# A linear-attention and gated-convolution kernel: negated filter spectrum read from PSUM, sign flips moved to VectorE, zero matmuls in pauses, and a new written-out order

## The chip, the cores and the metric

The kernel runs on one core of one Trainium2 chip. The metric is the device time of one execution in microseconds (us); the median of three executions is compared. TensorE (PE) does the matmuls, VectorE (DVE), ScalarE (ACT) and GpSimd (POOL) the elementwise work, and SyncE (SP) issues nearly all transfers.

## What is computed

The reference runs two blocks one after the other. Sizes are 4 batches, 8 heads, 768 time steps and head width 48, so a row of all heads is 384 wide.

```
for t in range(S):                                   # linear attention with decay
    cur = einsum('bhd,bhe->bhde', u * k_t, v_t)
    y[t] = einsum('bhd,bhde->bhe', r_t, state + cur)
    state = w_t[..., None] * state + einsum('bhd,bhe->bhde', k_t, v_t)
proj = y @ w_proj                                    # 384 -> 3 * 384: x1, x2, x3
x2_conv = irfft(rfft(x2, axis=time) * rfft(filter_fft, axis=time), n=S)
out = (x1 * x2_conv * x3) @ w_out
```

## The kernel before

The time axis is cut into chunks of 128 steps, six per batch, 24 in all (chunk 0 to 23). Loads and a part of the elementwise work go by group: chunks 0 and 1 alone, then pairs. For each chunk the names below are one operation each; a number behind the name is the chunk or the group.

- `lw`, `lk`, `lr`, `lv` (line 1244) are SyncE's loads of w, k, r and v, 192 KB each in runs of 192 bytes. `ln` (line 1250) is the logarithm of w on ScalarE. `vb` casts v to bf16.
- `rk`, `ru`, `rh`, `cc`, `vc` (lines 1158, 1260, 1263) make the bonus term: r times k, times u, a halving sum, a sum over the head, and that sum times v. They are spread over GpSimd and VectorE.
- `cs` (lines 1278 to 1281) sums the logarithms on TensorE, `ex` (1284) is the exponential on ScalarE in place in PSUM, `kq` (1287) multiplies with k and r on VectorE, `ph` (1291) is the decay of the whole chunk. `tr` (1299) transposes, `qk` copies the result out of PSUM (ScalarE or VectorE), `sc` (1311) are the scores, `mt` (1327, or a plain copy by line 1162) takes them out of PSUM with or without the causal mask, and `mc` (1332) cuts the triangle on GpSimd where `mt` was a plain copy.
- `ki`, `kv`, `su` (1358, 1352, 1362) carry the state to the next chunk: `su` on VectorE writes the state that `ys` (1381) of the next chunk reads. `yi`, `ys`, `y` add bonus, state part and scores part in PSUM; `xn` takes the sum out of PSUM (where `yi` is left out, `xn` on VectorE adds the bonus, line 1401); `yt` transposes and `xT` copies out.

For each batch the second block follows as soon as its rows are there: `xw` (1573) is the middle projection in natural layout and `cxw` its copy, `sd` (1584) folds the two halves of time, `f` (1438) is the forward transform with the sine table `F`, `cf` its copy to `X`. `p` and `q` (1536) are the other two projections: `cp` copies the first, `cq` (1561) makes their product, the gate `g`. `u` and `p` with two numbers (1158, 1610) multiply with the filter's spectrum `hh`. `E` (1628) is the inverse transform with the table `mi` and its sign-flipped copy `mx`, `cE`, `aE`, `dE`, `yE` put the halves together and multiply with the gate, `o` (1692) is the last projection, `co` its copy, `so` (1708) the store.

Three pieces are made once, in the first half of the run. The tables come from sines (`ang`, `ia`, `sin`, `is`). `if` (`flips`, lines 1481 to 1486) makes four sign-flipped copies of `mi` on GpSimd. The filter is loaded by `filt` (1495), folded by `fsd0` and `fsd1` (1498, VectorE, tile `P`), transformed by `h1`, `h2`, `h0` (1438), copied out of PSUM with its scale by `hc` on ScalarE (1504, tile `hh`), and `hg` (`gcopy`, lines 1508 to 1516) on VectorE makes the second copy and the negated one from the bf16 tile `hh`.

The order of all work is written out by hand in the table `ORDER`: one line per operation with its engine's letter (P TensorE, A, N ScalarE, D, V, M VectorE, G, C GpSimd, S SyncE, - for left out) and its PSUM bank. Each engine runs its own operations strictly in this order and waits at each for its inputs and its bank. A third word ties a GpSimd operation behind a VectorE one, if that one's function returns its instruction. `warm n` are n matmuls of a zero tile (line 1193).

Of the kernel before, what the change touches and what calls it, by code (L numbers as in the profile page):

```python
# [21 lines left out]
L = 128  # L22
NCH = S // L
C = H * D
# [13 lines left out]
ADD, DVE2, ACT2, POOL2, FOLD = "V", "M", "N", "C", "Q"  # L38
# [6 lines left out]
wz D  # L45
maps G
lw0 S
lr0 S
lk0 S
warm 30 7  # L50
lk1 S
lw1 S
smalls D
pads D
imaps G
ia0 G
kz3 D
kz1 D
ang2 D
u S  # L60
ang1 D
lw2 S
lw3 S
ang0 D
lr1 S
lr2 S
ia2 D
ia1 D
# [3 lines left out]
trig A  # L72
sin2 A
sin1 A
sin0 A
is A
table A
ln1 A
masks G ang0
ln0 A  # L80
rk0 G
ur D
um P 0
kz0 D
ub D
lv0 S
kz2 G ia2
cs1 P 4
rk1 G ia2
cs0 P 2  # L90
ln2 A
ex1 A
ru0 D
rh0 D
cc0 D
ex0 A
kq1 D
cs3 P 6
ex3 A
ph1 A  # L100
kq0 D
cs2 P 0
ex2 A
tr1 P 5
ph0 A
tr0 P 4
qk1 A
# [108 lines left out]
xn2 A
yt2 P 3
xT2 D
vb3 G su3
kv4 P  # L220
sc5 P 5
mt4.0 A
cc3 D
xT3 A
mt4.1 A
xw0.2 P 3
mt5.0 D
mt5.1 D
su4 D
mc4.1 G  # L230
cxw0.2 A
xw0.0 P 0
filt S
vc3 G xT2
yi5 P 5
mc5.1 -
ln4 A
cxw0.0 D
lv7 S
mc4.0 G mt5.0  # L240
yi4 P 3
ys5 P
ys4 P
y4 P
mc5.0 -
xn4 A
y5 P
xn5 D
cs6 P 0
lv6 S  # L250
lw9 S
yt4 P 2
xT4 D
yt5 P 5
xT5 D
cs7 P 3
ex6 A
lw8 S
ex7 A
kq6 D  # L260
xw0.4 P 6
kq7 D
ph6 A
cxw0.4 A
lk8 S
lr9 S
lv8 S
tr6 P 5
qk6 D
tr7 P 0  # L270
ph7 A
lr8 S
qk7 A
lk9 S
sd0.0.0 D
sc6 P 2
mt6.1 -
f0.0 P 6
lk10 S
wproj0 G  # L280
lv9 S
lw10 S
p0.2.1 P 4
p0.2.0 P 5
cf0.0 A
mt6.0 N
p0.0.1 P 0
rk4 D
sd0.1.0 D
cp0.2.0 D  # L290
f0.2 P 5
p0.0.0 P 2
cf0.2 A
cp0.0.0 A
sc7 P 6
lr10 S
lr11 S
lw11 S
ru4 D
cp0.0.1 D  # L300
fsd0 D
mc6.0 C
ln5 A
lk11 S
fsd1 D
h1 P 0
mt7.0 M
h2 P 2
lv10 S
mc6.1 -  # L310
rh4 D
cc4 D
mt7.1 -
hc1 A
hg1 D
mc7.0 -
h0 P 6
hc2 A
cp0.2.1 A
vb4 G xT4  # L320
vc4 G fsd0
lw13 S
lv13 S
kv6 P 3
hg2 D
su6 D
mc7.1 -
yi6 - 2
hc0 A
hg0 D  # L330
cs8 P 0
yi7 P 4
wproj2 G
y6 P
ys7 P
ex8 A
y7 P
xn6 V
cs9 P 6
xn7 A  # L340
ki7 P 2
kv7 P
kq8 D
yt7 P 3
yt6 P 5
tr8 P 4
su7 D
lr12 S
lv11 S
ex9 A  # L350
lr14 S
xT6 D
kq9 D
lw12 S
# [651 lines left out]
yE3.2.0 G cq3.2.0
o3.0.1 P
# [783 lines left out]
```

## Time and profile before

| what | before |
|---|---|
| time, median of three executions | 167.73 us (166.23 to 168.83) |
| profiled execution, its own time | 167.69 us |
| its span on the core | 165.9 us |
| mean granted TensorE clock | 0.931 |
| PE busy | 144.2 us (87%), 1665 matmuls |
| VectorE busy | 140.3 us (85%), 259 instructions |
| ScalarE busy | 117.7 us (71%), 192 instructions |
| GpSimd busy | 99.3 us (60%), 103 instructions |
| bytes moved | 26.23 MB, 158 GB/s over the span |

The page gives busy time by engine, then the span in 40 slices of 4.15 us. The view by windows gives the busy time of each engine in a stretch, so that an engine's idle time there is the difference. The waits name who ended the idle time. The profiled execution's own time is 1.79 us over its span.

### The profile page before, as it was taken

How to read it: one execution, taken by the hardware profiler on the slowest of the kernel's cores; microseconds unless marked ns; L12 is line 12 of the kernel's file. 1: busy time of each engine (PE TensorE's matmuls, PEld its weight loads, DVE VectorE, ACT ScalarE, POOL GpSimd, SP SyncE). 2: the span in 40 equal slices, each digit the busy share in tenths (PEclk: the TensorE clock that was granted, in tenths of full speed). 3: DMA queues.
4: the chain of work that ended last, by engine and by line, in shares of the span. 5: the costliest groups of instructions: out<-in, count | busy, mean ns of one | idle time of the engine just before them, and what ended most of it. 6: DMA issues, size and time to landing. Idle time of an engine off the chain costs nothing.

```text
span 165.9 us, 4290 instructions
## 1 busy us (share of the span) xinstructions
PE 144.2 (87%) x1665; PEld 94.9 (57%) x1665; DVE 140.3 (85%) x259; ACT 117.7 (71%) x192; POOL 99.3 (60%) x103
## 2 busy tenths in 40 slices
PE   7868877984984999649999999999989999999980
PEld 5538655652543667344666677667567666655530
DVE  6758999892799889375899999999999999999950
ACT  4997956674274686634998988878989866785460
POOL 7967796602227059985695799699269680330320
PEclk9965999998699599965999999999999999999997
DMA  5999999899999989999999999900250000200936
GB/s 107 212 212 215 207 199 203 161 287 194 211 212 175 203 166 205 184 217 214 201 192 217 191 211 184 175 11 0 96 194 0 4 0 4 95 2 19 356 133 254
DMA packets 104118, 26.23 MB, mean 158 GB/s; under 512 B 100129, under 2 KB 102690, under 8 KB 104098
## 3 DMA queue, kind: packets, MB, share of 16 engines
q1 hardware_dynamic: 102498, 24.78, 68.1%
q0 software_dynamic: 1600, 1.18, 5.0%
q8 instruction: 13, 0.21, 0.5%
q14 instruction: 7, 0.06, 0.1%
HBM read 22.41 MB, written 4.72 MB: 164 GB/s over the span
## 4 chain that ended last, share of the span: by engine, by line
PE 29%; DVE 22%; POOL 15%; DMA 12%; issue 11%; ACT 7%; SPq 1%; POOLq 0%; ACTq 0%; DVEq 0%
PE banks L1536 6%; POOL rk L1158 6%; DMA wproj<-in_moe_w_proj_dram 5%; PE banks L1438 5%; PE banks L1299 4%; DMA out_dram<-o 3%; PE banks L1692 3%; PE banks L1573 3%; POOL mt L1332 3%; DVE kq L1287 3%; PE banks L1628 2%; DVE hh L1514 2%; DMA w<-in_w_dram 2%; DMA kr<-in_k_dram 2%; POOL vc L1158 2%
## 5 line engine op out<-in xcount | busy, mean ns | idle before, releaser
L1536 PE MATMUL banks<-xT,wproj 128*128 128x384 bf16 x144 | 29.8, 344 | 2.7 <-DMA wproj<-in_moe_w_proj_dram 2.1
L1332 POOL TENSOR_SCALAR_AFFINE_SELECT mt<-mt 128x512 bf16<-128x512 bf16 (+1 forms) x17 | 15.9, 937 | 16.5 <-ACT mt L1162 11.8
L1158 POOL TENSOR_TENSOR vc<-vb,cc 128x768 bf16<-128x768 bf16 (+1 forms) x13 | 18.3, 1410 | 10.6 <-DVE cc L1263 7.6
L1287 DVE TENSOR_TENSOR kq<-banks,kr 128x768 bf16<-128x768 f32 x24 | 22.7, 950 | 2.2 <-ACT banks L1284 1.9
L1162 ACT ACTIVATE x<-banks 128x768 bf16<-128x768 f32 (+1 forms) x26 | 18.0, 700 | 6.1 <-PE banks L1573 4.0
L1158 POOL TENSOR_TENSOR rk<-kr 128x768 bf16<-128x768 f32 (+1 forms) x12 | 20.1, 1679 | 2.6 <-DMA kr<-in_r_dram 1.3
L1299 PE MATMUL banks<-ident,kq 128*128 128x128 bf16 x192 | 16.8, 243 | 5.1 <-DVE kq L1287 4.5
L1536 PEld LDWEIGHTS <-wproj 128*128 128x128 bf16 x144 | 13.5, 102 | 11.9 <-DMA wproj<-in_moe_w_proj_dram 2.5
L1284 ACT ACTIVATE banks<-banks 128x768 f32<-128x768 f32 x24 | 19.1, 804 | 0.5 <-PE banks L1281 0.2
L1299 PEld LDWEIGHTS <-kq 128*128 128x128 bf16 x192 | 13.6, 110 | 7.3 <-DVE kq L1287 6.7
L1327 DVE TENSOR_TENSOR mt<-banks,mask_excl 128x512 bf16<-128x512 f32 (+1 forms) x17 | 15.6, 934 | 2.4 <-PE banks L1311 2.0
L1162 ACT ACTIVATE qk<-banks 128x1024 bf16<-128x1024 bf16 x14 | 14.1, 1028 | 2.4 <-PE banks L1299 2.3
L1162 ACT ACTIVATE X<-banks 128x768 bf16<-128x768 f32 x12 | 9.7, 811 | 7.8 <-PE banks L1438 7.5
L1162 ACT ACTIVATE mt<-banks 128x512 bf16<-128x512 f32 (+1 forms) x17 | 12.6, 749 | 3.7 <-PE banks L1311 3.1
L1158 POOL TENSOR_TENSOR y<-y,g 128x768 bf16<-128x768 bf16 (+1 forms) x6 | 8.1, 1354 | 11.6 <-PE banks L1628 9.0
L1438 PE MATMUL banks<-sd,F 128*128 128x384 bf16 (+1 forms) x96 | 14.0, 336 | 0.3 <-DVE sd L1584 0.3
L1573 PE MATMUL banks<-wproj,xT 128*128 128x384 bf16 x72 | 14.0, 333 | 0.1
L1692 PE MATMUL banks<-wout,y 128*128 128x384 bf16 x72 | 13.2, 326 | 0.0
L1438 PEld LDWEIGHTS <-F 128*128 128x128 bf16 (+1 forms) x120 | 9.1, 106 | 7.0 <-issue 2.9
L1561 DVE TENSOR_TENSOR g<-banks,x 128x384 bf16<-128x384 f32 (+1 forms) x16 | 11.6, 747 | 0.2 <-PE banks L1536 0.2
L1162 ACT ACTIVATE o<-banks 128x768 f32<-128x768 f32 (+1 forms) x12 | 9.1, 782 | 3.6 <-PE banks L1692 1.9
L1158 DVE TENSOR_TENSOR U<-X,hh 128x2304 bf16<-128x2304 bf16 (+1 forms) x12 | 11.1, 950 | 0.0
(110 smaller groups left out, 331.0 us busy)
## 6 DMA issues: line engine op xcount, KB each, us to landing
w<-in_w_dram SPq DMA_DIRECT2D x24, 192.0 KB, 3.9
kr<-in_r_dram SPq DMA_DIRECT2D x24, 192.0 KB, 3.8
kr<-in_k_dram SPq DMA_DIRECT2D x24, 192.0 KB, 3.8
v<-in_v_dram SPq DMA_DIRECT2D x24, 192.0 KB, 4.2
out_dram<-o SPq DMA_DIRECT2D x11, 384.0 KB, 3.0
U<-in_moe_filter_fft_dram SPq DMA_DIRECT2D x1, 1152.0 KB, 9.3
wproj<-in_moe_w_proj_dram POOLq DMA_DIRECT2D x3, 288.0 KB, 5.8
out_dram<-o SPq DMA_DIRECT2D x2, 192.0 KB, 2.6
```

Of the source, the lines that this page charges most:

```text
L1158: return eng(e).tensor_mul(o, a, b)
L1162: return nc.scalar.activation(out=o, in_=a, func=AF.Copy)
L1284: op(f"ex{i}", [ACT], lambda e, bk: nc.scalar.activation(out=two(bk, f"cs{i}")[:, :, 0:C], in_=two(bk, f"cs{i}")[:, :, 0:C], func=AF.Exp), ...
L1287: op(f"kq{i}", [DVE], lambda e, bk: nc.vector.tensor_mul(kq[f][:, :, :, 0:D], two(bk, f"cs{i}")[:, :, 0:C].rearrange("p a (h d) -> p a h d ...
L1299: nc.tensor.transpose(p[:, HP * m + j, :], kq[f][:, m, 2 * j:2 * j + 2, :], ident)
L1327: return copy(ACT, o, x) if e in (ACT, ACT2) else nc.vector.tensor_mul(o, x, _mid(mask_excl, z - HP * a))
L1332: return nc.gpsimd.affine_select(out=o, in_=o, pattern=[[0, z - HP * a], [1, L]], compare_op=ALU.is_gt, fill=0.0, base=0, channel_multipli ...
L1438: nc.tensor.matmul(p[rows], F[:, ti, c0 + rows.start:c0 + rows.stop], x[q][:, ti, :], start=(ti == 0), stop=(ti == NT - 1),)
L1536: nc.tensor.matmul(p, wproj[:, cb, col0:col0 + L], xT[bx][:, cb, sl], start=(cb == 0), stop=(cb == CB - 1),)
L1561: op("c" + n3, [DVE], lambda e, bk: nc.vector.tensor_mul(g[bx][:, fs, sl], view(bk, n3), x1[:, fs, sl]), r=[f"x1.{fb}.{hf}" for fb in fbs] ...
L1573: nc.tensor.matmul(view(bk)[:, z], xT[bx][:, cb, (c0 + z) * L:(c0 + z + 1) * L], wproj[:, cb, C:2 * C], start=(cb == 0), stop=(cb == CB - 1),)
L1692: nc.tensor.matmul(view(bk)[:, z], yt_[:, z, :], wout[:, cb, :], start=(cb == 0), stop=(cb == CB - 1),)
```

## The change

Four edits are in the code, and the table of the order is new.

1. `hg` makes the negated part of the spectrum from PSUM instead of from the bf16 tile in SBUF, with the scale in the same instruction; for the first block the scale is a column `neg0`. Its other copies still go from `hh` to `hh`.
2. `if` stands in the table with VectorE's letter, and much earlier.
3. `warm` lines stand at many places: 73 zero matmuls where there were 30.
4. A new letter X takes `xn` out of PSUM on ScalarE into an fp32 tile `xf`, and a new GpSimd operation `xa` adds the bonus. Two chunks use it (18 and 20).

```diff
+    neg0 = sb.tile([L, 1], FP32, name="neg0")
+        nc.vector.memset(neg0, -2.0 / S)
+        nc.vector.memset(neg0[0:1, :], 0.0)
...
-            o = xn[:, i % NX].rearrange("p (j a d) -> p a j d", a=2, d=D)
+            o = (xf if e == WIDE else xn)[:, i % NX].rearrange("p (j a d) -> p a j d", a=2, d=D)
...
-            return copy(e, o, yview(bk))
+            return copy(ACT if e == WIDE else e, o, yview(bk))
...
+        op(f"xa{i}", [POOL, NONE], lambda e, bk: nc.gpsimd.tensor_add(
+            xn[:, i % NX], xf[:, i % NX], vcq.rearrange("p h d -> p (h d)")),
+           r=[f"xn.{i % NX}", f"vc.{fg}"], w=[f"xn.{i % NX}"])
...
                 nc.vector.tensor_scalar(
-                    out=hh[:, 1, 0, n, :], in0=hh[:, 0, 1, n, :], scalar1=-1.0, scalar2=None, op0=ALU.mult)
+                    out=hh[:, 1, 0, n, :], in0=two(bk, f"h{n}")[:, 1, 0:C], scalar1=-2.0 / S if n else neg0,
+                    scalar2=None, op0=ALU.mult)
...
-            op(f"hg{n}", [DVE], gcopy(n), r=[f"Hc.{n}"], w=[f"H.{n}"])
+            op(f"hg{n}", [DVE], gcopy(n), r=[f"Hc.{n}"], w=[f"H.{n}"], uses=[f"h{n}"])
```

Counted over the table, these operations change their engine: `qk` from 14 on ScalarE and 10 on VectorE to 16 and 8; `xT` from 11 and 13 to 17 and 7; `vb` from 7 on ScalarE and 6 on GpSimd to 10 and 3; `vc` from 13 on GpSimd to 11 and 2 on VectorE; `ru` and `rh` together from 15 on VectorE and 11 on GpSimd to 11 and 15; `yE` from 9 on VectorE and 6 on GpSimd to 12 and 3; `dE` from 8 and 4 to 11 and 3.

The first place is GpSimd around the loads of the projection's weights, `wproj` (the first of the two is the middle third, the second the first third). `vc2` and `rk0` belong to chunks 2 and 3 and to 4 and 5. Before:

```order
L1227 DMA wproj_137<-in_moe_w_proj_dram 128x3x384
L1158 TENSOR_TENSOR vc2_87<-vb2_83,cc2_80 128x768
L1158 TENSOR_TENSOR rk0_75<-kr3_67 128x768
L1164 CAST vb3_84<-v3_71 128x768
L1332 AFFINE_SELECT mt1_101<-mt1_101 128x512
L1158 TENSOR_TENSOR vc0_85<-vb3_84,cc0_78 128x768
L1332 AFFINE_SELECT mt1_101<-mt1_101 128x512
L1227 DMA wproj_137<-in_moe_w_proj_dram 128x3x384
```

Now:

```order
L1193 TENSOR_TENSOR vc2_87<-vb2_83,cc2_80 128x768
L1264 DMA wproj_138<-in_moe_w_proj_dram 128x3x384 x2
L1193 TENSOR_TENSOR rk0_75<-kr3_67 128x768
L1297 TENSOR_TENSOR rk0_75<-rk0_75 128x16x24
L1193 TENSOR_TENSOR vc0_85<-vb3_84,cc0_78 128x768
```

The first load moved behind `vc2`, and the second moved up behind it, ahead of `rk0`.

The second place is VectorE around the filter's spectrum: `P` is the folded filter, `hh` the spectrum, `S3` the state that `su6` writes. Before:

```order
L1498 TENSOR_TENSOR P_116<-U_117 128x1152 x2
L1327 TENSOR_TENSOR mt1_101<-banks_152,mask_excl_142 128x1024
L1260 TENSOR_TENSOR rk1_76<-rk1_76 128x16x24
L1263 TENSOR_REDUCE cc1_79<-rk1_76 128x16
L1510 COPY hh_136<-hh_136 128x384
L1514 TENSOR_SCALAR hh_136<-hh_136 128x384
L1510 COPY hh_136<-hh_136 128x384
L1514 TENSOR_SCALAR hh_136<-hh_136 128x384
L1362 TENSOR_TENSOR S3_106<-banks_152,phi2_94 128x192
```

Now:

```order
L1539 TENSOR_TENSOR P_117<-U_118 128x1152 x2
L1300 TENSOR_REDUCE cc1_79<-rk1_76 128x16
L1364 TENSOR_TENSOR mt1_101<-banks_154,mask_excl_143 128x1024
L1551 COPY hh_137<-hh_137 128x384
L1555 TENSOR_SCALAR hh_137<-banks_154 128x384
L1551 COPY hh_137<-hh_137 128x384
L1555 TENSOR_SCALAR hh_137<-banks_154 128x384
L1399 TENSOR_TENSOR S3_106<-banks_154,phi2_94 128x192
```

The negating instruction now reads the PSUM banks; the copies and their place stay.

The third place is VectorE some 10 us of work later, at `kq` of chunks 10 and 11 and the bonus of group 6 (`rk0`). Before:

```order
L1287 TENSOR_TENSOR kq3_91<-banks_152,kr2_66 128x16x48
L1158 TENSOR_TENSOR rk0_75<-rk0_75,u_b_151 128x768
L1287 TENSOR_TENSOR kq2_90<-banks_152,kr2_66 128x16x48
L1610 TENSOR_TENSOR P_116<-U_117 128x2304
L1263 TENSOR_REDUCE cc0_78<-rk0_75 128x16
```

Now:

```order
L1324 TENSOR_TENSOR kq3_91<-banks_154,kr2_66 128x16x48
L1324 TENSOR_TENSOR kq2_90<-banks_154,kr2_66 128x16x48
L1297 TENSOR_TENSOR rk0_75<-rk0_75 128x16x24
L1652 TENSOR_TENSOR P_117<-U_118 128x2304
L1300 TENSOR_REDUCE cc0_78<-rk0_75 128x16
```

The product with u (`ru6`) left VectorE for GpSimd and no longer stands between the two `kq`; the halving sum (`rh6`) came in behind them. GpSimd has the flips no more ahead of that group's `rk`: the four instructions of `if` now stand on VectorE right behind the product with u of chunks 4 and 5.

On TensorE the first projection of batch 0 (`p0.0.0`) now stands ahead of the transposes of chunks 4 and 5, of `xw0.4` and of `cs6`. Zero matmuls stand there in groups of two to six ahead of `xw0.0`, `xw0.4`, `sc6`, `sc7` and `h1`: 34 of them behind the 39 at the start.

More of the change, by code (lines that the diff above doesn't have):

```diff
@@ L45 @@
 wz D
[L46 to L53 removed]
+warm 28 5
+lw3 S
+lr0 S
+lw1 S
+lw0 S
+lk1 S
+trig A
+maps G
 pads D
 imaps G
[L56 to L68 removed]
+ia1 G
+u S
+lr1 S
+kz1 D
+smalls D
+ang2 D
+ang1 D
+ang0 D
+sin2 A
+ia0 D
+masks G ang0
+sin1 A
+lw2 S
+rk1 G ia0
+ia2 D
+lk0 S
+ur D
+um P 6
+warm 11 5
+kz2 D
+ub D
+ru1 D
+sin0 A
+is A
+table A
+kz3 D
 lk3 S
@@ L242 @@
[L242 to L256, printed above, removed]
-ex6 A
-lw8 S
+mt5.0 D
+mc5.0 -
+vc3 G
+warm 6 2
+xw0.0 P 2
+xw0.2 P 4
+mc4.0 C xT3
+rk4 G
+yi4 P 0
+yi5 P 6
+ys4 P
+ys5 P
+mc5.1 -
+y5 P
+lr8 S
+lk9 S
+cxw0.2 A
+mc4.1 -
+y4 P
+lr9 S
+lk8 S
+lv8 S
+lv9 S
+lr10 S
+p0.0.0 P 4
+xn4 A
+xa4 -
+yt4 P 1
+cxw0.0 D
+lw10 S
+lk10 S
+lw11 S
+xn5 D
+xa5 -
+yt5 P 3
+xT4 A
+xT5 D
+warm 3 2
+xw0.4 P 2
+cp0.0.0 D
+cxw0.4 D
+ln4 A
+cs6 P 4
+ex6 A
+sd0.0.0 D
@@ L259 @@
+kq6 D
+p0.2.1 P 7
+cs7 P 0
+p0.0.1 P 2
+cp0.2.1 A
 ex7 A
-kq6 D
-xw0.4 P 6
 kq7 D
 ph6 A
[L264 to L267, printed above, removed]
-tr6 P 5
[L269 to L276, printed above, removed]
-mt6.1 -
[L278 to L285, printed above, removed]
-mt6.0 N
[L287 to L309, printed above, removed]
-mc6.1 -
@@ L311 @@
[L311 to L317, printed above, removed]
-hc2 A
[L319 to L324, printed above, removed]
+cp0.0.1 A
+sd0.1.0 D
+ru4 D
+f0.0 P 6
+lr11 S
+lk11 S
+p0.2.0 P 4
+rh4 D
+cf0.0 A
+ph7 A
+tr7 P 3
+qk7 A
+tr6 P 5
+qk6 A
+cp0.2.0 A
+f0.2 P 6
+cf0.2 A
+lw12 S
+fsd0 D
+fsd1 D
+warm 5 2
+sc6 P 0
+ln5 A
+warm 6 2
+sc7 P 5
+cc4 D
+vb4 G fsd0
+mt7.0 M
+mc7.0 -
+mt7.1 -
+mt6.1 -
+lw13 S
+mt6.0 N
+warm 6 2
+h1 P 2
+h2 P 0
+hc1 A
+h0 P 4
+hg1 D
+mc6.1 -
+hc2 A
 hg2 D
+kv6 P 7
 su6 D
-mc7.1 -
@@ new lines @@
+cp2.0.0 A
+tr18 P 3
+vb10 A
+kq19 D
+ph19 A
+qk18 D
+xw2.2 P 6
+p2.2.0 P 1
+cxw2.2 A
+sc17 P 4
+mt17.1 A
+cp2.2.0 A
+ln11 A
+ru10 D
+mt17.0 D
+mc17.0 -
+vc9 G
+kv18 P 3
+q2.0.0 P 6
+su18 D
+cq2.2.0 D
+lr23 S
+lw23 S
+yi16 - 0
+ys16 P
+sc18 P 4
+mt18.1 -
+o0.0 P 2
+mt18.0 N
+rh10 G ru10
+cc10 D
+cq2.0.0 D
+co0.0 A
+mc16.1 G su18
+y16 P
+xn16 V
+xa16 -
+cs20 P 4
+mc17.1 G cq2.2.0
+tr19 P 6
+qk19 D
+yt16 P 3
+ex20 A
+mc18.1 -
+yi17 - 6
+o0.1 P 0
+vc10 G
+vb11 A
+mc18.0 C
+co0.1 A
+ys17 P
+y17 P
+xT16 D
@@ new lines @@
+sc19 P 2
+kq20 D
+mt19.1 -
+mc19.1 -
+ki19 P 1
+kv19 P
+xn17 V
+xa17 -
+ph20 A
+rk11 G
+yt17 P 7
+mt19.0 N
+tr20 P 4
+su19 D
+u01.0 D
+cs21 P 0
+ru11 D
+xT17 A
+qk20 A
+lw22 S
+rh11 G
+p1.0 D
+ex21 A
+xw2.4 P 5
+cxw2.4 A
+o0.2 P 2
+so0.0 S
+co0.2 A
+kq21 D
+p2.2.1 P 7
+ki20 P 6
+kv20 P
+su20 D
+sc20 P 4
+cp2.2.1 A
+p2.0.1 P 2
+q2.2.1 P 7
+mt20.0 D
+ln12 A
+mt20.1 A
+ph21 A
+cp2.0.1 A
+cs22 P 4
+ex22 A
+mc19.0 C
+tr21 P 6
+cc11 D
+yi18 - 2
+sd2.1.0 D
+lk23 S
+lk22 S
+y18 P
+mc20.0 -
+xn18 X
+q2.0.1 P 0
```

1279 lines of the change are left out of this document (592 added, 687 removed).

## The prediction

> **What bounds the kernel now.** I read the slices first, then the busy time by windows, then what VectorE waited for, and last the instructions around the long waits.
>
> ```profile
> PE   7868877984984999649999999999989999999980
> DVE  6758999892799889375899999999999999999950
> PEclk9965999998699599965999999999999999999997
> DMA  5999999899999989999999999900250000200936
> ```
>
> A slice is 4.15 us. Up to slice 25 (108 us) the transfers never pause, yet they are not what ends last: from slice 19 on TensorE and VectorE are both full, and they stay full for 58 us after the last input. Holes stand only before, at slices 8 to 10, 12, 13 and 16 to 18.
>
> ```profile
> core 0: us, PE busy (x) PEld busy (x) DVE busy (x) ACT busy (x) POOL busy (x), PEclk, DMA share, GB/s
> 12.00:33.30 21.30, 17.93 (x300) 13.89 (x299) 18.91 (x35) 15.28 (x29) 16.08 (x18) 0.89 1.04 197
> 33.30:80.25 46.95, 37.40 (x386) 23.27 (x385) 34.89 (x50) 27.34 (x44) 23.49 (x19) 0.85 1.03 206
> 80.25:161.70 81.45, 79.95 (x933) 52.11 (x931) 78.75 (x140) 65.54 (x109) 50.57 (x40) 1.00 0.47 112
> 50.90:54.30 3.40, 1.08 (x26) 0.87 (x26) 3.24 (x7) 0.89 (x2) 1.85 (x2) 1.00 1.10 169
> 54.30:57.70 3.40, 3.05 (x31) 2.24 (x27) 2.96 (x6) 2.13 (x4) 0.00 (x0) 0.50 1.13 215
> 68.00:71.40 3.40, 1.23 (x8) 0.52 (x6) 0.04 (x1) 1.08 (x2) 3.33 (x3) 1.00 1.07 209
> 71.40:78.20 6.80, 5.36 (x47) 3.53 (x47) 4.74 (x7) 3.23 (x5) 4.58 (x4) 0.50 1.10 217
> ```
>
> The run has three stages. In the last, from `kq` of chunk 12 at 80.25 us to the end of VectorE's work, TensorE is busy 79.95 of 81.45 us: nothing is to be had there but by taking work away. The middle one, 33.30 to 80.25, has 12.06 us without VectorE (46.95 less 34.89) and 9.55 without TensorE. So the question is how much earlier chunk 12 starts, and whether the last stage keeps its length. These are VectorE's waits in the middle stage:
>
> ```profile
> DVE x L1164 <- PE banks L1536: 4.0, 2, 3.1
> DVE rk L1158 <- POOL rk L1158: 3.7, 1, 3.7
> DVE mt L1327 <- PE banks L1311: 1.8, 1, 1.8
> DVE qk L1164 <- PE banks L1299: 0.3, 1, 0.3
> ```
>
> **The change part by part.**
>
> *a. The projection's weights.* The 4.0 us are `cp`, waiting for `p0` on TensorE, which waits for a transfer that GpSimd issues; the chain of waits has it as one piece of 8.62 us.
>
> ```profile
> 31.08 8.62 DMA wproj<-in_moe_w_proj_dram
> 24.19 1.82 POOL L1158 TENSOR_TENSOR rk<-kr 128x768 bf16<-128x768 f32 x1
> 30.78 0.88 SPq L1495 DMA_DIRECT2D U<-in_moe_filter_fft_dram  x1
> U<-in_moe_filter_fft_dram SPq DMA_DIRECT2D x1, 1152.0 KB, 9.3
> 43.91 2.62 DVE L1498 TENSOR_TENSOR P<-U 128x1152 bf16<-128x1152 f32 x2
> ```
>
> The changed order issues it ahead of the `rk` that starts at 24.19, so about 25 instead of 31; even at 8.62 us it lands by 34, when `p0.0.0` comes up. What is late next is the filter: issued at 30.78 and 9.3 us under way, it is there at 40.1 (estimate), so the fold `P` can move from 43.91 to 40.1 at best: 3.8 us. The changed order also puts `cp0.0.0`, `cxw0.4` and `sd0.0.0` ahead of `kq6`, some 2.5 us of work that VectorE had done behind it. I take 2.5; ends 0 (the weights are as late as before) and 3.8.
>
> *b. The negated spectrum.* On VectorE and GpSimd:
>
> ```profile
> 48.59 0.26 DVE L1510 COPY hh<-hh 128x384 bf16<-128x384 bf16 x1
> 48.77 1.53 DVE L1514 TENSOR_SCALAR hh<-hh 128x384 bf16<-128x384 bf16 x1
> 50.39 2.51 DVE L1514 TENSOR_SCALAR hh<-hh 128x384 bf16<-128x384 bf16 x1
> 52.82 0.34 DVE L1362 TENSOR_TENSOR S<-banks,phi 128x192 bf16<-128x192 f32 x1
> 53.96 0.26 DVE L1514 TENSOR_SCALAR hh<-hh 128x384 bf16<-128x384 bf16 x1
> 48.66 1.52 POOL L1158 TENSOR_TENSOR vc<-vb,cc 128x768 bf16<-128x768 bf16 x1 [5.91 <-DVE cc L1263]
> 50.96 1.81 POOL L1158 TENSOR_TENSOR rk<-kr 128x768 bf16<-128x768 f32 x1
> L1164 DVE CAST xn<-banks 128x384 bf16<-128x384 f32 x2 | 1.1, 552 | 0.1
> ```
>
> One and the same instruction takes 0.26 us where GpSimd is idle and 1.53 and 2.51 where `vc` and `rk` run: it ends at 50.30 and 52.90, just after they do (50.18 and 52.77). The two engines shut each other out there, for 3.5 us in sum. The state `S` stands behind it, and TensorE's pause from 50.90 to 54.30 follows from that. Read from PSUM, the nearest row of the size is 0.55, so three cost 0.9 more than 0.26 each: the gain is 2.6 if PSUM frees it, and 0 if the copies ahead of it, still from `hh` to `hh`, get shut out in its place. I take 2.4, nearer to the upper end since the one copy quoted took 0.26 with `vc` starting 0.07 later.
>
> The Trainium skill, SBUF — State Buffer, "Who interferes with whom", says the same of the lock, that the loser waits for the whole instruction; but it counts copies from SBUF among the instructions that contend. By that rule the four copies left in `hg` and the moved flips are as exposed as before; that is a rival below.
>
> *c. The flips.* GpSimd's rows:
>
> ```profile
> 64.73 1.25 POOL L1482 TENSOR_SCALAR mi<-mi,sgn 128x384 bf16<-128x384 bf16 x1
> 65.97 2.45 POOL L1484 TENSOR_SCALAR mx<-mi,sgn 128x384 bf16<-128x384 bf16 x2
> 68.40 1.16 POOL L1486 TENSOR_SCALAR mi<-mi 128x384 bf16<-128x384 bf16 x1
> 69.53 1.79 POOL L1158 TENSOR_TENSOR rk<-kr 128x768 bf16<-128x768 f32 x1
> 71.36 0.56 DVE L1158 TENSOR_TENSOR rk<-rk,u_b 128x768 bf16<-128x768 bf16 x1 [3.68 <-POOL rk L1158]
> ```
>
> The flips hold GpSimd for 4.9 us; `rk6` comes behind, VectorE's `ru6` waits 3.7 us for it, and `kq10` stands behind `ru6`. Without the flips `rk6` is done about 5 us sooner, and `ru6` has left that queue. I take the 3.7 whole. On VectorE four flips cost 1.0 at 0.26 each, and at most 8 at the 1.53 to 2.51 beside a busy GpSimd (estimate). They stand before `kq6`, where VectorE would wait for the filter in (a) anyway, so I count nothing; with that cover gone it is 1 to 2.
>
> *d. The clock.* At 54.30 and 71.40 the clock is granted at 0.50, each after a stretch in which TensorE worked 1.08 or 1.23 of 3.40 us. From 71.40 on, VectorE's waits for scores and transposes (1.8 and 0.3) and some small ones are of that half speed. Where b and c take the pauses away, no slow stretch follows: 2.3 us; ends 0 and 2.7, half of TensorE's 5.36 there. The Trainium skill, TensorE: Matmul & The Clock Gate, "What's actually happening", puts the fall after a whole idle window of some 3.4 us. This trace differs: about 1.1 busy of 3.40 was enough. By the rule alone zero matmuls would be needless in pauses as short as these.
>
> *e. Zero matmuls.* At the start 30 of them took 6.1 us:
>
> ```profile
> L1193 PE MATMUL banks<-wt 128*128 128x256 bf16 x30 | 6.1, 394 | 1.1 <-DVE scl L1208 1.1
> L1162 ACT ACTIVATE qk<-banks 128x1024 bf16<-128x1024 bf16 x14 | 14.1, 1028 | 2.4 <-PE banks L1299 2.3
> L1162 ACT ACTIVATE xT<-banks 128x384 bf16<-128x384 bf16 x11 | 5.3, 492 | 1.8 <-PE banks L1409 1.8
> L1162 ACT ACTIVATE vb<-v 128x768 bf16<-128x768 f32 (+1 forms) x7 | 5.6, 802 | 0.0
> ```
>
> That is 0.20 each at the slow start, so the 34 behind the start are at most 6.8 us. Seventeen stand before `sc6`, `sc7` and `h1`, where TensorE waits for the filter; of the other half I charge 0.5 (ends 0 and 3.4).
>
> *f. ScalarE.* Behind chunk 12 it takes four more `xT`, one more `qk`, one more `vb` and one `ev` less: 4 x 0.49 + 1.03 + 0.80 - 0.49 = 3.3 us. It had 15.9 idle in the last stage (81.45 less 65.54), so most is hidden; VectorE has about 1 us less there, but TensorE, the fuller one, the same. Since queues run in order, I charge half, 1.7 (ends -1, VectorE's work, and 3.3).
>
> The two chunks with `xa` only swap an eviction; the start trades `ia0` for `ia1` between two engines, within 1 us either way, and the early stage before 33.30 I leave as it is.
>
> **The sum.** 2.5 + 2.4 + 3.7 + 2.3 = 10.9. Holes do not close without new ones: the first stage, which lost nothing to these causes, still left VectorE idle 2.4 of 21.30. I take 1.5 for that. 10.9 - 1.5 - 0.5 - 1.7 = 7.2. The span goes from 165.9 to 158.7, and with the 1.79 around it (167.69 less 165.9) to 160.5. The profiled execution is the median of the three, 167.73, to 0.04. The inputs do not stop this: the last `kq` but one runs at
>
> ```profile
> 122.90 0.88 DVE kq L1287
> ```
>
> and the transfers pause from 108 on, 15 us before.
>
> **The rivals.**
>
> *The lock stays* (0.15). GpSimd's operations around `hg` are not tied to it: `gcopy` returns no instruction, so the third word after `hg1` and `hg2` does nothing. If `mc6.0` and `rk5` run beside the copies, these wait as the negations did: b gives 0, the pause follows and half of d goes (1.1). 160.5 + 2.4 + 1.1 = 164.0. Against it: the copy of 0.26 above.
>
> *The pauses come back elsewhere* (0.20). `p0.0.0` now stands ahead of `yt4`, `xw0.4` and `cs6` on TensorE. If its weights land late, everything behind waits, and VectorE's `kq6` with it; the filter gets later too. Then a gives 0 and d half: 160.5 + 2.5 + 1.1 = 164.1, with another 1.5 of new waits 165.6: no change that can be told. For it: a is the largest wait of the stage; against it, the issue 6 us sooner.
>
> *ScalarE becomes the bound, slower* (0.06). In the last stage ScalarE gets 3.3 us more in an order where TensorE is at 98%. If each moved eviction holds a bank until ScalarE comes round to it, TensorE stalls. Without its term the forecast is 158.8; it decides against the change from 8.9 us on, and seven stalls like the 1.8 above would be 12.6: 171.4. Against it: in 33.30 to 80.25 VectorE's waits on ScalarE are too short for the four rows quoted.
>
> **How the numbers follow.** Forecast 0.59, with 156 to 163.5 as its own range: all upper ends, 3.8 + 2.6 + 3.7 + 2.7 and the 1 of VectorE's work, make 13.8 without new waits, or 153.9. About 2% (3.4 us) is what a measurement of this kernel can tell from no change; faster means below 164.4, slower above 171.1. Faster: 0.57 of the forecast, 0.10 of the lock, 0.08 of the pauses, 0.75. Slower: 0.04 of ScalarE and 0.02 of the pauses, 0.06. The rest, 0.19, is no change. The range, 155.5 to 167, takes in the lock and the pauses and leaves out the far upper ends and ScalarE.
>
> **What would show it.** Right: `P` starts by 42; the negations take 0.5 to 0.6 each; no wait of several us of VectorE on GpSimd's `rk`; clock at 1.00 between 45 and the end; `kq` of chunk 12 at 71 to 73; the stage behind it 80 to 83 long. Wrong: copies of `hh` over 1 us, a pause at `p0.0.0`, a last stage over 85, or chunk 12 still at 78.

## The result, and the profile after

The changed kernel takes 160.57 us, the median of four executions (159.55 to 162.07), against 167.34 us (166.23 to 168.83): 0.9596 of before, with a 95% interval of 0.9507 to 0.9685. The forecast was 160.5. The profiled execution took 160.61 us with a span of 158.9, where the sum had 158.7, and a mean clock of 0.979 against 0.931. The sum came out to 0.2 us; its terms did not. Here and below the ratios leave out executions more than 1.5% above the fastest of their kernel, the medians do not.

These rows of the slices answer to those of before. A slice is 3.97 us here.

```profile
PE   7767978399999599889999999999999999999990
DVE  6849979823996999999999999989999999799960
PEclk9999999659999999999999999999999999999999
DMA  5999899999799999899999989908740002200746
```

Behind the start one large group of holes is left, at slices 7 to 9 (28 to 40 us), with smaller ones at 12 and 13. Where before had four slow stretches there is one, and it lies in the large group. From slice 13 on VectorE is full. The windows cut the run as the prediction did, with the slow stretch and the window ahead of it as rows of their own.

```profile
core 0: us, PE busy (x) PEld busy (x) DVE busy (x) ACT busy (x) POOL busy (x), PEclk, DMA share, GB/s
12.00:34.26 22.26, 16.99 (x255) 11.60 (x254) 17.71 (x32) 14.63 (x28) 15.82 (x15) 0.89 1.06 197
34.26:75.60 41.34, 38.48 (x468) 24.91 (x466) 35.85 (x52) 30.89 (x51) 19.85 (x15) 0.98 1.04 209
75.60:155.10 79.50, 78.34 (x928) 51.64 (x926) 76.17 (x139) 68.55 (x115) 51.48 (x42) 1.00 0.54 128
25.98:29.39 3.41, 1.76 (x29) 1.08 (x27) 3.12 (x9) 0.76 (x2) 1.22 (x2) 1.00 1.28 208
29.39:36.20 6.81, 5.70 (x28) 3.24 (x28) 2.79 (x5) 1.78 (x3) 3.04 (x3) 0.50 1.04 220
```

`kq` of chunk 12 starts at 75.60 against 80.25, and the last stage is 79.50 us long against 81.45. VectorE has 76.17 busy in it (78.75 before), TensorE 78.34 (79.95), ScalarE 68.55 (65.54). VectorE's waits in the middle stage are these:

```profile
DVE x L1199 <- PE banks L1615: 2.7, 2, 2.4
DVE xn L1199 <- PE banks L1426: 2.0, 1, 2.0
DVE hh L1551 <- ACT hh L1545: 1.3, 1, 1.3
DVE xT L1199 <- PE banks L1450: 1.0, 1, 1.0
DVE xn L1438 <- POOL mt L1369: 0.3, 1, 0.3
```

The 4.0 us behind the projection's weights and the 3.7 behind GpSimd's `rk` are gone. New is a wait for `xw` (line 1615) and, behind it, one for `y` (1426), both work that TensorE did late. The same piece as the chain of waits and TensorE's list of instructions show it:

```profile
22.58 7.00 DMA v<-in_v_dram
```

```profile
27.35 0.39 PE L1228 MATMUL banks<-wt 128*128 128x256 bf16 x2
30.50 0.41 PE L1389 MATMUL banks<-vb,kq 128*64 128x48 bf16 x8 [2.75 <-ACT vb L1197]
30.84 1.46 PE L1228 MATMUL banks<-wt 128*128 128x256 bf16 x6
32.09 4.05 PE L1615 MATMUL banks<-wproj,xT 128*128 128x384 bf16 x12
```

`v` of chunk 4 lands only at 29.58; ScalarE casts it, and TensorE's `kv4` (line 1389) waits 2.75 us. In the window 25.98 to 29.39 TensorE worked 1.76 of 3.41 us, and from 29.39 on the clock is granted at 0.50 for 6.81 us. Two zero matmuls stand ahead of this pause and six behind it; none lies in it, and the six take 1.46 us at half speed. `y4` starts at 37.02, before at 31.32.

### The profile page after: what moved, and what is told of

It reads as the page before. It is cut to its first block, busy times and chain, and to the rows that moved or that the text cites. A ratio compares the mean times of both kernels' runs of the same rounds, so it can differ in the third digit from the quotient of the medians.

```text
span 158.9 us, 4371 instructions
## 1 busy us (share of the span) xinstructions
PE 142.5 (90%) x1706; PEld 94.2 (59%) x1706; DVE 137.6 (87%) x259; ACT 123.1 (77%) x203; POOL 95.9 (60%) x96
## 4 chain that ended last, share of the span: by engine, by line
PE 45%; DVE 22%; ACT 12%; DMA 8%; issue 5%; SPq 4%; POOL 2%; DVEq 0%; ACTq 0%; POOLq 0%
PE banks L1578 8%; PE banks L1734 7%; PE banks L1615 7%; PE banks L1479 6%; DMA v<-in_v_dram 4%; PE banks L1670 4%; DVE kq L1324 4%; SPq L1281 4%; DMA w<-in_w_dram 3%; ACT qk L1197 3%; PE banks L1336 2%; DVE U L1193 2%; PE banks L1228 2%; ACT vb L1197 2%; DVE g L1603 2%
## 5 line engine op out<-in xcount | busy, mean ns | idle before, releaser
L1193 POOL TENSOR_TENSOR rk<-kr 128x768 bf16<-128x768 f32 (+1 forms) x13 | 22.7, 1746 | 5.9 <-DMA kr<-in_k_dram 2.6
L1193 POOL TENSOR_TENSOR vc<-vb,cc 128x768 bf16<-128x768 bf16 x11 | 16.6, 1511 | 13.7 <-DVE cc L1300 10.7
L1197 ACT ACTIVATE qk<-banks 128x1024 bf16<-128x1024 bf16 x16 | 16.3, 1022 | 0.4
L1364 DVE TENSOR_TENSOR mt<-banks,mask_excl 128x1024 bf16<-128x1024 f32 (+1 forms) x17 | 16.3, 965 | 0.0
L1369 POOL TENSOR_SCALAR_AFFINE_SELECT mt<-mt 128x512 bf16<-128x512 bf16 (+1 forms) x16 | 13.8, 869 | 3.9 <-ACT mt L1197 1.4
L1336 PE MATMUL banks<-ident,kq 128*128 128x128 bf16 x192 | 14.2, 219 | 1.8 <-DVE S L1399 1.2
L1336 PEld LDWEIGHTS <-kq 128*128 128x128 bf16 x192 | 11.4, 97 | 3.5 <-DVE kq L1324 2.3
L1228 PE MATMUL banks<-wt 128*128 128x256 bf16 x73 | 12.4, 326 | 1.1 <-DVE wt L1250 1.1
L1193 POOL TENSOR_TENSOR rk<-rk,u_b 128x768 bf16<-128x768 bf16 (+1 forms) x7 | 12.2, 1739 | 0.4
L1603 DVE TENSOR_TENSOR g<-banks,x 128x768 bf16<-128x768 f32 (+1 forms) x16 | 11.7, 749 | 0.1
```

Source lines behind the costliest of these rows:

```text
L1193: return eng(e).tensor_mul(o, a, b)
L1197: return nc.scalar.activation(out=o, in_=a, func=AF.Copy)
L1228: nc.tensor.matmul(banks[:, at, 0:256], wt[:, 0:L], wt, start=True, stop=True)
L1336: nc.tensor.transpose(p[:, HP * m + j, :], kq[f][:, m, 2 * j:2 * j + 2, :], ident)
L1364: return copy(ACT, o, x) if e in (ACT, ACT2) else nc.vector.tensor_mul(o, x, _mid(mask_excl, z - HP * a))
L1603: op("c" + n3, [DVE], lambda e, bk: nc.vector.tensor_mul(g[bx][:, fs, sl], view(bk, n3), x1[:, fs, sl]), r=[f"x1.{fb}.{hf}" for fb in fbs] ...
```

## The experiments

Unless said otherwise an edit is to the changed kernel, and no edit changes what is computed. Beside a time stands its ratio to the kernel before on the same chip.

**Where the gain comes from: the flips.** `if` goes back to GpSimd, ahead of `rk6`, all else as changed.

```diff
-if D
 ...
+if G
 rk6 G
```

> The changed kernel with the four flips back on GpSimd, ahead of rk of chunks 10 and 11. Theory (the flips on GpSimd were what held chunks 10 to 12): rk6 starts 4.9 us later than the 63.74 of the changed kernel, the halving sum rh6 on VectorE waits 3 to 4 us for GpSimd, kq of chunk 12 starts 2.5 to 5 us later, span 161.5 to 164. Rival (the new order as a whole made the gain, and has room for the flips): kq of chunk 12 within 1 us of 75.6, span within 1 us of 158.9.

Measured: 165.70 us (163.91 to 168.36), ratio 0.9871 [0.9775, 0.9967], span 164.0. GpSimd's instructions, then VectorE's wait, then two windows:

```profile
64.98 2.88 POOL L1525 TENSOR_SCALAR mx<-mi,sgn 128x384 bf16<-128x384 bf16 x2
67.83 1.16 POOL L1527 TENSOR_SCALAR mi<-mi 128x384 bf16<-128x384 bf16 x1
68.97 1.81 POOL L1193 TENSOR_TENSOR rk<-kr 128x768 bf16<-128x768 f32 x1
```

```profile
DVE rk L1297 <- POOL rk L1193: 3.5, 1, 3.5
```

```profile
71.35:74.76 3.41, 0.37 (x9) 0.19 (x8) 2.23 (x3) 1.14 (x2) 1.91 (x2) 1.00 1.10 213
74.76:81.59 6.83, 5.73 (x55) 3.66 (x56) 5.38 (x9) 3.20 (x6) 5.67 (x6) 0.50 0.90 175
```

With one line moved the picture of before returns: `rk6` at 68.97 instead of 63.74, a wait of 3.5 us behind it, a window with 0.37 of 3.41 us of TensorE, and 6.83 us at half clock. From `kq` of chunk 8 to that of chunk 12 it takes 25.19 us; the changed kernel takes 19.95 and before 25.65. By the medians this one line is worth 5.1 us (165.70 less 160.57) of the 6.8. In the profiled execution the clock also fell at 54.28. The changed kernel can have that too: its repeat, below, fell at 53.95 and takes 21.23 us for the same piece. Against that execution the line is worth 4.0.

**Is the negation from PSUM worth anything?** It reads SBUF again.

```diff
-  in0=two(bk, f"h{n}")[:, 1, 0:C], scalar1=-2.0 / S if n else neg0,
+  in0=hh[:, 0, 1, n, :], scalar1=-1.0,
```

> The changed kernel with the negation read from the bf16 tile in SBUF again. Prediction's step b: 2.4 us were gained by PSUM, so the span would be 161 or more. Theory after the result (the copies ahead are shut out by GpSimd in place of the negations): one of the six instructions still waits for rk5 until it ends, the others take 0.26, so su6 and the span stay within 0.7 us, perhaps below, as 0.26 is less than 0.55.

Measured: 160.76 us (156.36 to 162.32), ratio 0.9611 [0.9481, 0.9742]: nothing lost that these times can tell. Its profiled execution, span 154.7, is the first without a slow stretch before 155 us. From the first operation of `hg` to `kq` of chunk 8 it takes 4.39 us, less than the changed kernel's 4.91, with one negation of 1.44 beside GpSimd. The kernel with zero matmuls in the pause, which comes below, negates from PSUM and takes 4.38, so the 0.5 need not be the negation's.

**Are the zero matmuls worth anything?** All 34 behind the start are left out.

```diff
-warm 2 2
 kv4 P
 ...
-warm 6 2
 xw0.0 P 2
```

> The changed kernel without the 34 zero matmuls behind the start (39 at the start stay). Theory (they hold the clock between 36 and 50 us): a second half-speed stretch shows between 36 and 55 us, kq of chunk 8 starts 1 to 3 us later, span 160 to 162. Rival (they only stand in TensorE's way): no new half-speed stretch, kq of chunk 8 0.5 to 1.5 us earlier, span 157.5 to 158.5.

Measured: 160.49 us (157.88 to 161.55), span 158.7. `v` of chunk 4 lands at 30.75, TensorE works 1.70 of 3.41 us, and the clock falls at 29.12 for 6.83 us, as in the changed kernel. Where they stand the zero matmuls neither cost nor bring anything that these runs tell.

**Zero matmuls in the pause.** 26 of them stand ahead of `kv4`, none behind.

```diff
-warm 2 2
+warm 26 2
 kv4 P
-warm 6 2
 xw0.0 P 2
```

> The changed kernel with 26 zero matmuls ahead of kv4, where TensorE waits from 27.35 to 30.44 us for a cast, in place of 2 ahead of it and 6 behind it. Theory (that pause drops the clock to one half from 29.4 to 36.2, and xw of batch 0 runs at half speed in it): clock at 1.00 there, y of chunk 4 3 us earlier than 37.0, kq of chunk 8 2 to 3 us earlier than 55.65, span 156 to 157. Rival (the filter or the transfers hold that stage anyway): the clock stays up but kq of chunk 8 within 0.7 us, span within 0.7 us.

Measured: 159.75 us (157.27 to 162.65), ratio 0.9425 [0.933, 0.952], span 155.6. TensorE's list and the window of the pause:

```profile
27.39 3.01 PE L1227 MATMUL banks<-wt 128*128 128x256 bf16 x26
30.33 0.31 PE L1388 MATMUL banks<-vb,kq 128*64 128x48 bf16 x8
30.57 2.12 PE L1614 MATMUL banks<-wproj,xT 128*128 128x384 bf16 x12
```

```profile
27.28:30.69 3.41, 3.41 (x43) 2.77 (x36) 3.03 (x9) 1.75 (x2) 1.74 (x2) 1.00 1.28 218
```

`kv4` is as late as before (30.33). Here it stands behind the zero matmuls, since the cast of `v` was done at 29.61. But the window is full, the clock stays at 1.00, the twelve `xw` matmuls take 2.12 us instead of 4.05, `y4` starts at 33.48 against 37.02 and `kq` of chunk 12 at 72.28 against 75.60. So it was the slow stretch, not the late `v` alone, that cost the 3.3 us; about 0.5 of them lie at `hg`, where the longest copy took 1.30 here and 2.00 there. The medians overlap with the changed kernel's: two of the four executions had a mean clock of 0.958 and 0.974, so a stretch elsewhere; the two at 0.994 and 1.0 have spans of 155.6 and 156.3.

**What is locked out?** The copies of the real spectrum read PSUM too.

```diff
-  nc.vector.tensor_copy(out=hh[:, 1, 1, n, :], in_=hh[:, 0, 0, n, :])
+  nc.vector.tensor_scalar(out=hh[:, 1, 1, n, :], in0=two(bk, f"h{n}")[:, 0, 0:C],
+      scalar1=2.0 / S if n else scl0, scalar2=None, op0=ALU.mult)
```

> The changed kernel, but the copies of the real spectrum read PSUM too (with the scale), so that none of VectorE's six spectrum operations reads and writes SBUF at once. In the changed kernel the copy at 51.82 us took 2.00 us beside GpSimd's rk5 and another 0.49. Theory (what is locked out is an operation with its input and output in SBUF while GpSimd works): every one of the six takes 0.5 to 0.6 us, the stretch from the first of them (hg1) to kq of chunk 8, 4.91 us in the changed kernel, falls to 3.4 to 3.8, the span by about 1.2. Rival (GpSimd's float32 work locks VectorE out whatever it reads): one operation of 1.5 to 2 us remains there and the stretch stays at 4.7 to 5.1.

Measured: 156.49 us (154.70 to 158.78), ratio 0.9368 [0.9247, 0.9488], span 155.5. The changed kernel's rows on VectorE and GpSimd, then this kernel's on VectorE:

```profile
51.15 0.55 DVE L1555 TENSOR_SCALAR hh<-banks 128x384 bf16<-128x384 f32 x1
51.82 2.00 DVE L1551 COPY hh<-hh 128x384 bf16<-128x384 bf16 x1
53.74 0.55 DVE L1555 TENSOR_SCALAR hh<-banks 128x384 bf16<-128x384 f32 x1
```

```profile
51.88 1.81 POOL L1193 TENSOR_TENSOR rk<-kr 128x768 bf16<-128x768 f32 x1
```

```profile
47.96 0.55 DVE L1559 TENSOR_SCALAR hh<-banks 128x384 bf16<-128x384 f32 x1
48.56 0.56 DVE L1551 TENSOR_SCALAR hh<-banks 128x384 bf16<-128x384 f32 x1
49.03 0.55 DVE L1559 TENSOR_SCALAR hh<-banks 128x384 bf16<-128x384 f32 x1
```

In the changed kernel the negations, from PSUM, take 0.55, and the copy between them, SBUF to SBUF, takes 2.00: it ends at 53.82, just behind GpSimd's `rk5` (53.69). Here `rk5` runs from 48.62 to 50.44, over two of these rows, and they take 0.55 each. The three main copies and two longer negations take 0.55 to 0.61. The stretch to `kq` of chunk 8 is 4.02 us, 0.9 less: the theory holds, short of its 3.4 to 3.8. The median is lower by more than that, 4.1 us. The kernel before took 0.9 less beside it (166.47), and the clock had a part in the rest: in this execution it fell at 21.61 for 3.41 us and not at 29, and two of the four had a mean clock of 0.996 and 1.0.

**Why is `v` of chunk 4 late?** The second half of the projection's weights is issued behind `rh3`.

```diff
-wproj0 G
 ...
 rh3 G ru3
+wproj0 G
```

> The changed kernel, but the second half of the projection's weights is issued after the r-hat of chunk 3 (about 28.4 us) and not at 23.3. Theory (the early weights are what made v of chunk 4 late, 7.0 us under way): v lands 1 to 2 us sooner, kv4 starts by 29.3 against 30.5, there is no stretch at clock 0.50 at 29 to 36, y4 starts at 33 to 34 against 37.0, the projection p0.0.0 then waits for the weights until 35 to 36, and the span is 155 to 157.5. Rival (v is late from the load of all queues): kv4 stays at 30 to 31.5, the clock falls as before, and the span is 158.5 to 161.

Measured: 157.82 us (156.92 to 158.37), ratio 0.9523 [0.9424, 0.9623], span 155.8. `v` is there in time and the clock stays:

```profile
26.43 0.84 ACT L1197 ACTIVATE vb<-v 128x768 bf16<-128x768 f32 x1 [0.18 <-DMA v<-in_v_dram]
```

That looked like proof, but the kernel with three edits, below, issues these weights late too, and its cast starts at 29.33. In the runs of the new order it starts anywhere from 26.43 to 30.77 us. Whether the weights delay `v` is left open; that the pause with the slow clock is what costs here is not.

**Who bounds the last stage?** Four evictions go back to VectorE.

```diff
-xT10 A
+xT10 D
```

and the same for `xT11`, `xT14` and `xT20`.

> The changed kernel, with the evictions xT of chunks 10, 11, 14 and 20 on VectorE again, as in the kernel before. Theory (TensorE and VectorE set the last stage, ScalarE's 68.55 busy of 79.50 us has room): VectorE gets 4 x 0.35 = 1.4 us more and the last stage, from kq of chunk 12 to the last VectorE work, is 80 to 81 us against 79.50. Rival (ScalarE had become what the last stage waits for, the term f of 1.7 us): it is 78 to 79.

Measured: 160.92 us (159.27 to 162.90), ratio 0.9678 [0.9571, 0.9784], span 159.3. The last stage, taken from `kq` of chunk 12 to the last store, is 82.62 us against 79.83: 2.8 longer, twice what was expected. One operation explains the excess, here on VectorE, with GpSimd's beside it:

```profile
96.32 3.65 DVE L1193 TENSOR_TENSOR U<-X,hh 128x2304 bf16<-128x2304 bf16 x1
```

```profile
95.26 0.91 POOL L1297 TENSOR_TENSOR rk<-rk 128x384 bf16<-128x384 bf16 x1
96.93 1.82 POOL L1193 TENSOR_TENSOR rk<-kr 128x768 bf16<-128x768 f32 x1
```

In the changed kernel this `U` takes 1.35 us. Moved by the four evictions it meets GpSimd's `rk` and takes 3.65, 2.3 more; that leaves 0.5 for the evictions themselves. ScalarE is not the bound, since the stage got no shorter with less on it. TensorE is the fullest engine of the stage, and VectorE's delay shows as idle time of TensorE: 3.88 us against 1.49 in the changed kernel. Most of it is one wait, for an `xT`:

```profile
PE banks L1578 <- DVE xT L1199: 1.9, 1, 1.9
```

**How much is the code, how much the order?** Before's order, with the negation from PSUM and the flips on VectorE.

```diff
 ru3 D
+if D
 ...
-if G
 rk6 G
```

> The kernel before with its own order, with two edits of the change alone: the spectrum's negation read from PSUM, and the sign flips on VectorE right behind ru of chunk 3 (they were on GpSimd ahead of rk of chunk 6). Theory (the flips' place carries the gain, the new order little): rk6 starts about 5 us sooner than at 69.5, no stretch at clock 0.50 at 71 to 78, kq of chunk 12 at 75 to 76.5 against 80.25, span 160.5 to 162. Rival (the new order of the whole middle part carries it): kq of chunk 12 stays at 78 or later and the span is 163.5 to 166.

Measured: 162.78 us (162.71 to 163.60), ratio 0.9834 [0.9756, 0.9912], span 161.9, `kq` of chunk 12 at 76.27. In this kernel the third part of the negated spectrum is another quantity: `kv6` takes over its PSUM bank ahead of `hg2`. The next kernel has `hg2` ahead of `kv6`.

> The kernel before with its own order and the two edits (negation from PSUM, flips on VectorE behind ru of chunk 3), now with the third part of the spectrum's negation put ahead of kv of chunk 6, which takes its PSUM bank. In the run without that, kq of chunk 12 came at 76.27 and the span was 161.9. Theory (the two edits give some 4 us, the new order another 3): kq of chunk 12 at 75.5 to 77, span 160.5 to 162.5. Rival (kv6 waiting behind the negation opens a pause of TensorE's and the clock falls): kq of chunk 12 at 78 or later, span 163 or more.

Measured: 162.89 us (161.66 to 165.11), ratio 0.9724 [0.9642, 0.9806], span 160.0.

```profile
34.52 7.25 DMA wproj<-in_moe_w_proj_dram
```

```profile
74.08:156.04 81.96, 80.02 (x934) 52.10 (x932) 78.51 (x140) 65.62 (x109) 50.67 (x40) 1.00 0.56 132
```

The theory holds: the two edits give 5.1 us and the new order another 2.9. In the profiled executions they part by stage. The two edits do all of the middle: `kq` of chunk 12 starts at 74.08, sooner than in the changed kernel, though the first projection still waits for its weights until 41.81. The new order gives its gain in the last stage: to the last store it takes 81.96 us here and 81.79 before, against 79.83.

**The three cures together, and one lock more.** These ran beside the changed kernel itself.

> The changed kernel itself once more, as the measure for the three beside it. By the first runs: median 159.5 to 161.5 us, mean clock 0.97 to 0.98, one stretch at clock 0.50 near 29 to 36 us. If an execution comes without such a stretch, its span should be 154 to 156 us, as the one execution of the kernel with the spectrum negated from SBUF that had none (154.7).

Measured: 159.99 us (158.31 to 162.71, six executions), ratio 0.9541 [0.9467, 0.9616], clock 0.958 to 0.979. The profiled one had two slow stretches, the second behind `hg`:

```profile
26.64:30.05 3.41, 1.70 (x31) 1.10 (x28) 3.41 (x9) 1.72 (x3) 0.98 (x2) 1.00 1.27 196
30.05:33.46 3.41, 3.41 (x14) 1.82 (x13) 1.59 (x4) 0.41 (x1) 2.46 (x2) 0.50 1.04 205
50.54:53.95 3.41, 1.74 (x35) 1.17 (x34) 3.28 (x8) 1.73 (x4) 1.22 (x1) 1.00 1.07 155
53.95:57.36 3.41, 3.41 (x32) 2.54 (x31) 3.11 (x6) 2.38 (x5) 0.00 (x0) 0.50 1.18 228
```

> The changed kernel with three single edits together: the zero matmuls moved into TensorE's pause (26 ahead of kv4, none behind), the spectrum's copies read from PSUM, the second half of the projection's weights issued after the r-hat of chunk 3. Theory (each takes away another part: no stretch at clock 0.50, no copy over 0.7 us, v of chunk 4 not late): kv4 by 28.5, kq of chunk 12 at 70.5 to 71.5, span 154 to 155, median 155.5 to 157. Rival (the three cure one and the same pause, and zero matmuls and late weights then only add): span 155.5 to 156.5, as with one of them alone.

Measured: 157.35 us (156.42 to 158.00), ratio 0.9414 [0.9361, 0.9466], span 155.8, `kq` of chunk 12 at 72.50, `kv4` at 30.49. The rival holds: the three cure one pause, and by the spans they are together no faster than the late weights alone (155.8). The zero matmuls even hold `kv4` back by 0.3 us, as its cast was done at 30.17. From the fastest to the slowest of six it is 1.6 us, against 4.4 of the changed kernel; the late weights alone had 1.5 in four.

The last kernel adds one edit to these three:

```diff
+u00.0 D
-rk6 G
+rk6 G u00.0
 ...
-u00.0 D
```

> The kernel with the three edits together, and the product U of the second transform put ahead of GpSimd's rk of chunk 6, which waits for it. In the changed kernel that U took 2.90 us beside rk6 (63.87 and 63.74 us) and 1.36 elsewhere. Theory (VectorE is locked out by GpSimd's float32 product): U takes 1.36, kq of chunk 12 comes 1.0 to 1.5 us sooner than with the three edits alone, the span falls by as much. Rival (rk6 and what stands behind it, 1.4 us later, are then waited for, or the next operation of VectorE is locked out in its place): kq of chunk 12 within 0.4 us of the kernel with three edits, or later.

Measured: 156.95 us (155.59 to 159.37), ratio 0.9372 [0.931, 0.9434], span 155.5. The changed kernel's row, then this kernel's:

```profile
63.87 2.90 DVE L1193 TENSOR_TENSOR U<-X,hh 128x2304 bf16<-128x2304 bf16 x1
```

```profile
61.17 1.38 DVE L1192 TENSOR_TENSOR U<-X,hh 128x2304 bf16<-128x2304 bf16 x1
```

`U` takes 1.38, and from `kq` of chunk 8 to that of chunk 12 it is 18.96 us instead of 19.95: the theory's 1.0. The medians, 0.4 apart, do not tell the two kernels apart. In this execution the 26 zero matmuls keep `kv4` until 32.01, 2.1 us after its cast was done (29.94).

## Why the prediction was right, and where it was not

The net came out, 7.0 us of span against 7.2, but that was luck: wrong terms of opposite sign met. From `kq` of chunk 8, which starts at 54.60 before and 55.65 after, the run parts into three pieces: up to it 1.05 us lost where a and b had 4.9 gained; from it to chunk 12 25.65 to 19.95, 5.7 gained where c and d had 6.0; the last stage 1.95 gained where f had 1.7 lost. Another 0.4 lies behind VectorE's last work, and 2.0 had been set aside for e and for new waits. Of the signs that were to show the forecast right, `kq` of chunk 12 came at 75.60 and not at 71 to 73, and the last stage took 79.50 and not 80 to 83; one sign of being wrong, a copy of `hh` over 1 us, was there.

*a. The projection's weights: its wait went, and the next thing late was the wrong one.* No wait at `p0.0.0` is left, but the prediction named the filter as what is late next, and it was `v` of chunk 4, with a slow clock behind it. `P` starts at 45.22 where "by 42" was to show the step right. In the five profiles with no slow stretch ahead of it, it starts at 41.49 (negation from SBUF) to 43.68 (the last kernel), against 43.91 before. So 0.2 to 2.4 of the 2.5 were there to be had, and in the changed kernel the pause took them.

*b. The negated spectrum: the rival "The lock stays" was right.* The negations take 0.55, as forecast, and the lock moved to the copy of 2.00. Beside the changed kernel the run with the negation from SBUF is no slower. The 2.4 was 0 within what the runs tell: in before's own order, with the negation from PSUM, the stretch from the first copy to `kq` of chunk 8 takes 5.7 us against 6.0. The rival's second half, a slow stretch behind `hg`, came in the repeat and not in the first profile. The evidence I weighed against the rival, one copy of 0.26 with `vc` starting 0.07 behind it, was of a copy that had begun before GpSimd's instruction. The Trainium skill, SBUF — State Buffer, "Who interferes with whom", counts copies from SBUF among the contenders; the 2.00 agrees, and the 0.55 of the reads from PSUM beside `rk5` fits it too.

*c. The flips: right.* 3.7 forecast, and 3.5 came back as a wait when they went back. On VectorE they take 1.84 us instead of 1.0 (one beside GpSimd's `rh3`), at a place where it cost nothing that the runs show.

*d. The clock: right in the middle, wrong about the start.* "Clock 1.00 between 45 and the end" holds in every slice of this profile; the repeat of the kernel had a fall at 53.95. With it the repeat takes 21.23 us from `kq` of chunk 8 to that of chunk 12, so c and d together gave 4.4 there and 5.7 in the first profile. The stretch at 29.39 was not foreseen: the step looked only for the pauses that close, and 1.76 of 3.41 us was little enough for the clock to fall, as 1.08 and 1.23 had been. The Trainium skill's rule that the prediction set beside this, a fall after a whole idle window, differs from these runs; by it the 26 zero matmuls in the pause would have brought nothing, and they brought 3.3 us.

*e. Zero matmuls: 0.5 charged, 0 within what the runs tell.* They stood beside the pause, not in it. In it `kq` of chunk 12 came 3.3 us sooner.

*f. ScalarE: wrong sign.* I charged what ScalarE gets, let VectorE's loss count for at most 1, and took TensorE's work as the same. It was not: TensorE's busy time in the stage fell by 1.61 us (79.95 to 78.34), the stage by 1.95. Part of it can be named: one `yi` fewer (6 to 4 matmuls), and 12.3 us for the matmuls of `E` instead of 12.7. VectorE's busy time fell by 2.6. Groups of VectorE's last stage, before and after:

```profile
L1260 DVE TENSOR_TENSOR rk<-rk 128x384 bf16<-128x384 bf16 x3 | 3.0, 1008 | 0.0
L1164 DVE COPY xT<-banks 128x384 bf16<-128x384 bf16 x7 | 2.5, 351 | 0.4 <-ACT banks L1284 0.2
```

```profile
L1199 DVE COPY xT<-banks 128x384 bf16<-128x384 bf16 x3 | 1.1, 351 | 0.2 <-PE banks L1450 0.2
L1297 DVE TENSOR_TENSOR rk<-rk 128x384 bf16<-128x384 bf16 x1 | 0.3, 347 | 0.0
```

The prediction counted the four `xT`, 1.4 us. It missed that two `rh` go to GpSimd and that those on VectorE had been locked out there: 1.01 us each where the one left takes 0.35. That is 2.7 us more. ScalarE does not set the stage, and VectorE does so only where TensorE comes to wait for it: to the last store TensorE was idle 1.84 us before and 1.49 after, which leaves 0.35 of the 1.95 to shorter waits. The kernel with the flips back points to TensorE too. Its last stage begins with 1.84 us at half clock; VectorE is as busy as in the changed kernel (76.30), TensorE is 1.04 us busier, and the stage, 80.78, is 0.95 longer. So most of the gain goes with TensorE's shorter work. No run changes that work alone, so this is not proved.

The 1.5 for new waits was meant for just such a thing as `v` of chunk 4; that piece cost about 3.3.

## What to carry to other kernels

When one wait of an in-order engine is removed, look in the order for every load that stands near it, not only for the one that you know to be late: a pause of 2.7 us brought a slow stretch worth about 3. Place zero matmuls between the late input's neighbours, where the engine really waits, or leave them out, and no more of them than the wait needs: 26 kept the clock up, and held back the work behind them by 0.3 to 2.1 us where the input was there first. Before moving an operation on VectorE, ask which GpSimd instruction will run beside its new time: an SBUF-to-SBUF operation may wait that instruction out, and one that reads PSUM did not.

## What the runs showed of the hardware

- The clock is judged in windows of 3.41 us that run on by themselves: within a run all slow stretches start a multiple of 3.41 apart. Where they lie against the program differs between executions, and so one kernel's time does: in the changed kernel the pause at `hg` fell across two windows, the first with 2.89 us of work, and nothing came of it; in its repeat the window from 50.54 had 1.74, and the clock fell.
- The clock fell without a wholly idle window. Of 18 falls in all these profiles, the one at the end of each run left out, 15 came behind 0.37 to 1.83 us of work in 3.41, and 2.00 and 2.28 were survived (two windows of the kernel with the negation from SBUF). The line is not sharp: by the same records three falls came behind 1.9 to 2.5, and four windows with 1.4 to 1.95 passed.
- The lock between VectorE and GpSimd hits operations with both ends in SBUF: copies (0.26 to 2.00, once 2.62), products (1.35 to 2.90 and 3.65) and sums (0.35 to 1.71). It does not hit all of them: `cc`, the sum over the head, took 0.53 to 0.55 us each time, beside GpSimd or not. `kq`, which reads PSUM, took 0.93 to 0.96 in all 336 executions of the 14 profiles, most of them beside GpSimd. GpSimd pays too: `ru6`, in the same place, took 2.64 us where `U` ran into it and 1.64 where it did not.
